# The last softmax chain of a fused attention and mixture kernel, written in another order

## The chip, the cores and the metric

The kernel runs on one core of a Trainium2 chip. The metric is device time in microseconds (us) from the launch to the end of the program. TensorE (PE) multiplies, VectorE (DVE), ScalarE (ACT) and GpSimd (POOL) work element by element, and SyncE (SP) only issues DMA transfers, in the order in which they stand in the program.

## The reference

Three layers follow each other. Attention has 4 batches, 8 heads, 576 positions and 64 values a head; each query keeps its 32 highest scores. Its output, 2304 tokens of 512 values, goes through a soft mixture: 32 slots (8 experts with 4 slots each) are filled by a softmax over all tokens, each expert runs its slots through two matrices, and every token takes its mean of the slots back. The last layer is a dense one with 2048 hidden values.

```
logits = x @ phi                              # 2304 x 32
d = exp(logits - logits.max(0)); d /= d.sum(0) + 1e-09
slot_input = (d.T @ x).reshape(8, 4, 512)
h = maximum(slot_input[e] @ w1[e], 0); slot_out[e] = h @ w2[e]
c = exp(logits - logits.max(1)); c /= c.sum(1) + 1e-09
x = c @ slot_out
h = x @ w_in; g = where(h >= 1, h, where(h <= -1, 0, (h + 1)**2 / 4)); out = g @ w_out
```

## The kernel before

Attention works on 16 pairs of heads, four pairs to a batch. A frame of small operations, written by hand as a list of tokens (ORDER), is repeated; the list TAIL gives the order of the last frames. A token such as `A40.15` is an operation (A: product of the turned weights with v), a row block (4), a head (0) and a pair (15). Each engine does its instructions strictly in that order.

The softmax over tokens runs along: after each batch the 32 columns of logits give a new running maximum, `acc` (the slots' inputs, 128 x 128) is scaled by `al`, the ratio of old to new exponential, and the batch's own product is added. The first three batches do this in quarters while attention goes on. The last batch cannot: its rows come out of the last pair. So `last_mix` handles it in three pieces of 256, 256 and 64 columns (n = 0, 1, 2). Each piece has steps with a letter each: a and b are the products with phi (b is the last of four), c copies the logits from PSUM to the tile lT, d takes the maximum, l copies the logits to lall, e is the exponential, f is al, t turns the exponentials, g copies them to SBUF, w weighs x with them, x adds into acc, and y keeps the running sum. Tokens are `n`, letter and piece: `nb1.15`. All three pieces live in one PSUM tile, `lm_ps`, one bank each.

The framework that builds the program keeps the order of accesses to a tile, not to a bank: where an access to `lm_ps` on one engine follows one on another engine in the list, it waits for it, even where the banks differ. This can be read from the semaphore counts of the built program.

Around the chain stand `fl4` (the 64 last tokens of the last pair turned), `xc` (their copy to xT), `H4` (the rows scaled), `jp`/`jd` (running sums joined), then `sp` (acc turned into si_ps) and `sa` (copied to siT). The expert layer starts with siT: `ex_in(0)`, `ex_in(1)` multiply it with w1 (128 products of 512 columns), `ex_out(0)`, `ex_out(1)` with w2, `m_first` and the loop over steps make the last layer.

The weights come through a ring of SBUF slots of 512 KB. SP issues a load when its slot is free, and there are eight semaphores in turn, so at most eight loads are under way. Here the loads are numbered: w_0 to w_31 are w1; w_32 to w_37 and w_40 to w_65 are w2 (w_50 to w_65 for `ex_out(1)`); w_38 and w_39 are the first two tiles of w_out; w_66 and later are w_in and the rest of w_out. Some slots (wB) take the place of tiles that only attention uses, such as the work pool p_work, so their first load waits for the last use of what lay there. w_38, w_39 and w_40 to w_44 go to such slots.

Of the kernel before, what the change touches and what calls it, by code (L numbers as in the profile page):

```python
# [26 lines left out]
NSLOT = 32  # L27
# [8 lines left out]
NR = 4  # L36
REM = S - NR * P
# [72 lines left out]
def kernel_body(tc, qT, kT, vP, phi, w1, w2, w_in, w_out, out, fast, flag):  # L110
    nc = tc.nc
# [9 lines left out]
    acc = cpool.tile([P, P], F32, name="acc")  # L121
# [81 lines left out]
    p_work = att.enter_context(tc.tile_pool(name="p_work", bufs=2))  # L203
# [290 lines left out]
    last_ps = {}  # L494
# [249 lines left out]
    def last_mix(k, n):
# [8 lines left out]
        turned = bank[:, :(NR + 1) * NSLOT].rearrange("p (r s) -> p r s", s=NSLOT)  # L753
        pu = bank[:, 2 * P:3 * P]
        if k in "ab":
            for c in range(NHP - 1) if k == "a" else (NHP - 1,):
                nc.tensor.matmul(lg, phi_sb[:, c].rearrange("p g s -> p (g s)"), xs[c][1][:, c0:c1],
                                 start=(c == 0), stop=(c == NHP - 1), skip_group_check=True)
        elif k == "c":
            nc.scalar.copy(lT[:, c0:c1], lg)  # L760
        elif k == "d":
            mb = p_moe.tile([P, 1], F32, name="mb", tag="mb", bufs=3)
            nm = p_moe.tile([P, 1], F32, name="nmn", tag="nmn", bufs=4)
            nc.vector.reduce_max(mb, lT[:, c0:c1], axis=AX.X)
            nc.vector.scalar_tensor_tensor(nm, mb, -1.0, nrun[0], op0=ALU.mult, op1=ALU.min)
            sums[n] = dict(old=nrun[0], nm=nm)
            nrun[0] = nm
        elif k == "l":
            own = slice((B - 1) * NSLOT, B * NSLOT)
            nc.vector.tensor_copy(lall[own, c0:c1], lT[own, c0:c1])  # L770
        elif k == "e":
            sb = p_moe.tile([P, 1], F32, name="sb", tag="sb", bufs=3)
            nc.scalar.activation(eT[:, c0:c1], lT[:, c0:c1], AF.Exp, bias=sums[n]["nm"], scale=1.0, accum_out=sb)
            sums[n]["sb"] = sb
        elif k == "f":
            al = p_moe.tile([P, 1], F32, name="al", tag="al", bufs=3)
            nc.scalar.activation(al, sums[n]["old"], AF.Exp, bias=sums[n]["nm"], scale=-1.0)
            sums[n]["al"] = al
        elif k == "t":
            eye = ident[:NSLOT, :NSLOT]  # L780
            for r in main:
                nc.tensor.transpose(turned[:, r, :], eT[:NSLOT, r * P:(r + 1) * P], eye)
            if mid:
                for jj in range(2):
                    sl = slice(jj * REM, (jj + 1) * REM)
                    flip(turned[sl, NR, :], eT[:NSLOT, NR * P:], eye, jj)
        elif k == "g":
            if mid:
                for jj in range(2):
                    sl = slice(jj * REM, (jj + 1) * REM)  # L790
# [25 lines left out]
    def emit(name, pi):  # L816
        k = name[0]
        if k == "l":
            op_late(pi, name[1])
        elif k == "z":  # L820
            if 0 < pi < NPAIR - 1:
                load_pair(pi + 1)
        elif k == "m":
            if pi % NHP == NHP - 1:
                op_moe(pi, k)
        elif k in "cd":
            if k == "c" or pi < NWE:
                i = pi + min(pi, NWE) + (k == "d")
                if i < NCV:
                    conv_op(i, int(name[1]))  # L830
                    if (i, name[1]) == (NCV - 1, "6"):
                        wfree.extend(cv_slots)
                        wload(99)
        else:
            if name == "G00" and pi > 0:
                return
            if name == "S00":
                wload(2)
            if pi == NPAIR - 1 and last_pair(name, pi):
                return  # L840
            calls[k]((pi, int(name[1])), *([int(name[2])] if len(name) > 2 else []))
# [48 lines left out]
    def emit_tail(tok):  # L890
        name, pi = tok.split(".")
        pi = int(pi)
        if name[:2] in special and pi == lastp:
            special[name[:2]]((pi, int(name[2])))
        elif name[0] == "n":
            last_mix(name[1], int(name[2]))
        elif name[0] == "j":
            join(name[1])
        elif name in ("sp", "sa"):
            slots_in(name[1])  # L900
        else:
            emit(name, pi)
        freed(tok)
# [545 lines left out]
```

## Time and profile before

| | us |
|---|---|
| median of 3 runs | 773.34 (772.63 to 773.79) |
| the profiled execution | 771.83 |
| its span, first to last instruction | 770.0 |

| engine | busy us | share of the span |
|---|---|---|
| PE | 736.8 | 96% |
| DVE | 651.0 | 85% |
| ACT | 612.2 | 80% |
| POOL | 491.7 | 64% |

Attention takes the first 480 us or so, the experts stand from 490 to 530 us, and the last layer fills the rest. The shares are means over all stages. The change lies between 477 and 490 us, and what it is worth is read there and in the expert stage behind it.

### The profile page before, as it was taken

The numbers are of one execution on the slowest core, as the hardware profiler recorded it, in microseconds if no ns is written. First come the engines' busy times: TensorE is split into PE (matmuls) and PEld (weight loads), VectorE is DVE, ScalarE is ACT, GpSimd is POOL, SyncE is SP. The second block draws the span as 40 slices with busy tenths as digits, with TensorE's granted clock in tenths as the row PEclk, the third lists the DMA queues.
The fourth block names the chain that finished last, engine by engine and source line by source line (L and its number), as shares of the span: only waits on it lengthen the run. The fifth ranks groups of instructions, "written<-read, shape, count | busy, mean of one in ns | idle before, by whom it ended". The sixth has DMA issues, their size and how long they took to land.

```text
span 770.0 us, 15917 instructions
## 1 busy us (share of the span) xinstructions
PE 736.8 (96%) x5014; PEld 542.5 (70%) x5014; DVE 651.0 (85%) x2924; ACT 612.2 (80%) x1300; POOL 491.7 (64%) x532
## 2 busy tenths in 40 slices
PE   4899999999999999999999999898999999999996
PEld 2477777677777677777777788334577788888885
DVE  5999999999999999999999996173899967776662
ACT  4799999999999999999999997243788864554542
POOL 2899999999999999999999995030455400000000
PEclk9899999999999999999999999899999999999998
DMA  7414314304304302202202137999600020100101
GB/s 230 144 59 149 105 47 150 132 25 150 129 22 151 136 19 96 83 15 96 82 20 96 46 105 273 334 406 406 269 0 1 0 83 1 43 10 33 41 1 45
DMA packets 32013, 81.50 MB, mean 106 GB/s; under 512 B 5680, under 2 KB 6576, under 8 KB 31920
## 3 DMA queue, kind: packets, MB, share of 16 engines
q1 hardware_dynamic: 31632, 79.94, 29.1%
q8 instruction: 41, 0.67, 0.4%
q10 hardware_dynamic: 288, 0.46, 0.2%
q14 instruction: 52, 0.43, 0.2%
HBM read 71.25 MB, written 8.91 MB: 104 GB/s over the span
## 4 chain that ended last, share of the span: by engine, by line
PE 58%; DVE 24%; POOL 7%; DMA 6%; issue 2%; ACT 1%; SPq 1%; DVEq 0%; POOLq 0%; ACTq 0%
PE o_ps L1255 19%; PE av_ps L550 10%; PE s_ps L333 6%; PE pt_ps L509 6%; DVE cand L357 5%; DVE top L463 4%; DMA w<-in_moe_w_dram 3%; PE x_ps L333 3%; DVE ghl L1239 3%; POOL ssb L489 3%; DVE cand L362 2%; DVE top L364 2%; POOL mb L416 2%; PE av_ps L548 2%; PE h_ps L1207 2%
## 5 line engine op out<-in xcount | busy, mean ns | idle before, releaser
L1255 PE MATMUL o_ps<-whl,ghl 128*128 128x512 f32 x864 | 216.9, 395 | 1.3 <-DVE ghl L1221 0.5
L1255 PEld LDWEIGHTS o_ps<-whl,ghl 128*128 128x128 f32 x864 | 160.2, 188 | 38.1 <-DVE whl L1201 2.6
L489 POOL TENSOR_TENSOR ssb<-ssb,pen 128x576 f32<-128x576 f32 x141 | 180.3, 1283 | 2.9 <-ACT pen L486 0.4
L357 DVE MAX8 cand<-ssb 128x8 f32<-128x82 f32 (+1 forms) x1008 | 163.7, 235 | 5.4 <-ACT ssb L348 5.4
L550 PE MATMUL av_ps<-v_sb,ptb 128*128 128x65 f32 (+1 forms) x1280 | 143.0, 262 | 0.0
L550 PEld LDWEIGHTS av_ps<-v_sb,ptb 128*128 128x128 f32 (+1 forms) x1280 | 137.1, 181 | 6.3 <-issue 6.2
L1210 ACT ACTIVATE rg<-h_ps,half 128x384 f32<-128x384 f32 (+1 forms) x98 | 56.0, 572 | 68.3 <-PE h_ps L1207 68.3
L333 PE MATMUL s_ps<-kt,qt 64*128 64x288 f32 x512 | 99.5, 466 | 8.7 <-ACT ssb L348 4.4
L416 POOL TENSOR_SCALAR mb<-ssb,top 128x576 bf16<-128x576 f32 x62 | 106.9, 1724 | 0.9 <-DVE top L364 0.9
L348 ACT COPY ssb<-s_ps 128x576 f32<-128x576 f32 x144 | 95.4, 663 | 10.7 <-PE s_ps L333 9.5
L509 PE MATMUL pt_ps<-ident,ssb 128*128 128x128 f32 x600 | 93.8, 279 | 1.9 <-ACT ptb L525 1.8
L509 PEld LDWEIGHTS pt_ps<-ident,ssb 128*128 128x128 f32 x600 | 67.0, 146 | 29.5 <-ACT rs L533 6.8
L1227 DVE SCALAR_TENSOR_TENSOR rg<-h_ps,rg 128x384 f32<-128x384 f32 x95 | 52.7, 555 | 36.4 <-ACT rg L1211 36.3
L492 ACT ACTIVATE ssb<-ssb,kn 128x576 f32<-128x576 f32 x94 | 76.6, 816 | 0.1
L525 ACT COPY ptb<-pt_ps 128x512 f32<-128x512 f32 x120 | 73.0, 608 | 2.3 <-PE pt_ps L509 2.1
L486 ACT ACTIVATE pen<-ssb,kn 128x576 bf16<-128x576 f32 x94 | 73.8, 809 | 1.2 <-POOL kn L482 0.5
L463 DVE MAX8 top<-x_ps 128x8 f32<-128x584 f32 x94 | 71.1, 758 | 3.2 <-PE x_ps L447 2.8
L1190 POOL TENSOR_SCALAR tr_l<-tr_l 128x512 f32<-128x512 f32 x16 | 24.1, 1503 | 77.3 <-DVE tr_l L1189 77.3
L364 DVE MAX8 top<-cand 128x8 f32<-128x56 f32 x432 | 73.0, 206 | 0.1
L1239 DVE TENSOR_TENSOR ghl<-rg,ghl 128x384 fp32r<-128x384 f32 x95 | 67.7, 713 | 5.7
L453 POOL TENSOR_TENSOR w<-ssb,mb 128x576 f32<-128x576 f32 x50 | 64.6, 1293 | 1.2 <-DVE mb L413 1.2
L333 PEld LDWEIGHTS s_ps<-kt,qt 64*128 64x128 f32 x512 | 39.9, 190 | 34.6 <-ACT ssb L348 10.7
(246 smaller groups left out, 1307.2 us busy)
## 6 DMA issues: line engine op xcount, KB each, us to landing
w<-in_moe_w_dram SPq DMA_DIRECT2D x50, 512.0 KB, 6.7
x<-in_moe_w_in_dram SPq DMA_DIRECT2D x16, 512.0 KB, 3.8
w<-in_moe_w_out_dram SPq DMA_DIRECT2D x16, 512.0 KB, 10.3
w<-in_moe_w_dram SPq DMA_DIRECT2D x28, 256.0 KB, 5.7
kt<-in_k_dram SPq DMA_DIRECT2D x15, 360.0 KB, 4.3
v_sb<-in_v_dram SPq DMA_DIRECT2D x16, 325.0 KB, 6.8
qt<-in_q_dram SPq DMA_DIRECT2D x15, 320.0 KB, 5.0
out_dram<-o_sb SPq DMA_DIRECT2D x17, 256.0 KB, 2.3
```

Source lines behind the costliest of these rows:

```text
L333: nc.tensor.matmul(o, q[us], k[us, c:c + o.shape[-1]], start=True, stop=True, tile_position=(j * D, 0), skip_group_check=True)
L348: nc.scalar.copy(ssb[:, 0] if u[1] == NR else ssb[:, :, hf], st.pop((u, hf))[:, :, :HS])
L357: nc.vector.max(st[u]["cand"][:, j, 8 * g:8 * g + 8], row(u, j)[:, S * g // NSEG:S * (g + 1) // NSEG])
L364: nc.vector.max(t8, cand)
L416: nc.gpsimd.tensor_scalar(kept(u, j), row(u, j), t_u, None, op0=ALU.is_ge)
L463: nc.vector.max(st[u]["top"][:, j, TOPU:], src)
L489: nc.gpsimd.tensor_tensor(row(u, j), row(u, j), st.pop((u, "pen", j)), op=ALU.subtract)
L492: nc.scalar.activation(row(u, j), row(u, j), AF.Exp, bias=st[u]["kn"][:, j, 0:1], scale=0.125)
L509: nc.tensor.transpose(pt[:, c, :], pr[:, c0:c0 + P], ident)
L550: nc.tensor.matmul(o, pj[:, c, sl], v_sb[:, 4 * jj + c, :], start=False, stop=(c == NR - 1), skip_group_check=True)
L1239: nc.vector.tensor_tensor(gl, g, gh.bitcast(F32), op=ALU.subtract)
L1255: nc.tensor.matmul(pos[t][n], a[:, sl], w, start=(f == 0 and k == 0), stop=(f == NF - 1 and k == 2))
```

## The change

The order of the last 70 tokens or so is new, and some steps change.

- Maximum and exponential read the logits from PSUM, not from lT. The copies of pieces 1 and 2 to lT (for lall) are moved to the end of the chain.
- The products of piece 1 with phi are split into single tokens (`na10`, `na11`, `na12`); those of piece 2 stand ahead of the last product with v (`A40`).
- The copies of the turned exponentials of pieces 0 and 1 go from ACT to DVE. Piece 2 has one copy into a new tile e_mid, not two into er.
- Piece 2 is not weighed into lm_ps and added to acc any more. `dg` makes the diagonal matrix `grown` with piece 2's al; `sp` multiplies acc with it, which turns and scales in one, and piece 2's eight products of 64 x 32 add to si_ps there.
- `grown` is a tile of p_work (the tag rs).
- Nine bf16 products of 512 columns (`k4`, `k2`, `k3`), whose result nobody reads, stand in three places of PE's order.

```diff
-Q41.15 R4.15 nb0.15 nc0.15 nd0.15 nl0.15 fl3.15 fl2.15 A40.15 xc2.15 A41.15 rd4.15 na1.15 ne0.15
...
+Q41.15 R4.15 nb0.15 nc0.15 nd0.15 nl0.15 fl3.15 fl2.15 na2.15 A40.15 xc2.15 A41.15 rd4.15 na10.15
+na11.15 ne0.15 xc3.15 H4.15 nf0.15 fl4.15 na12.15 xc4.15 nb1.15 nd1.15 nb2.15 nt0.15 ne1.15 nd2.15
...
     def slots_in(k):
-        if k == "p":
+        if k == "g":
+            last_ps["g"] = p_work.tile([P, P], F32, name="grown", tag="rs", bufs=3)
+            nc.vector.tensor_scalar(last_ps["g"], ident, sums[len(pieces) - 1]["al"], None, op0=ALU.mult)
+        elif k == "p":
             last_ps["s"] = ps_m.tile([P, P], F32, name="si_ps", tag="m_ps")
-            nc.tensor.transpose(last_ps["s"], acc, ident)
+            nc.tensor.matmul(last_ps["s"], acc, last_ps["g"], start=True, stop=True, skip_group_check=True)
...
-            nc.vector.reduce_max(mb, lT[:, c0:c1], axis=AX.X)
+            nc.vector.reduce_max(mb, lg, axis=AX.X)
...
-            nc.scalar.activation(eT[:, c0:c1], lT[:, c0:c1], AF.Exp, bias=sums[n]["nm"], scale=1.0, accum_out=sb)
+            nc.scalar.activation(eT[:, c0:c1], lg, AF.Exp, bias=sums[n]["nm"], scale=1.0, accum_out=sb)
...
         elif k == "g":
             if mid:
-                for jj in range(2):
-                    sl = slice(jj * REM, (jj + 1) * REM)
-                    nc.scalar.copy(er[sl, jj, :], turned[sl, NR, :])
-            if main:
-                lo, hi = main[0], main[-1] + 1
-                nc.scalar.copy(et[:, lo:hi], turned[:, lo:hi])
+                nc.scalar.copy(e_mid, turned[:, 0, :])
+            else:
+                nc.vector.tensor_copy(et[:, main[0]:main[-1] + 1], turned)
         elif k == "w":
-            weigh(pu, xs, et, main, mid)
+            if mid:
+                si = last_ps["s"]
+                for hp in range(NHP):
+                    for jj in range(2):
+                        sl = slice(jj * REM, (jj + 1) * REM)
+                        nc.tensor.matmul(si[sl, hp * NSLOT:(hp + 1) * NSLOT], xs[hp][0][sl, 8, :], e_mid[sl],
+                                         start=False, stop=True, skip_group_check=True)
+            else:
+                weigh(pu, xs, et, main, False)
...
+        elif name[0] == "k":
+            for _ in range(int(name[1:])):
+                nc.tensor.matmul(last_ps["t"][:, 0], nbig, ident.bitcast(BF16).unsqueeze(1).to_broadcast([P, 2, 2 * P]),
+                                 start=True, stop=True, skip_group_check=True)
```

On PE, from the last turning of scores to the turning of piece 0's exponentials, the program stood before like this (L757 are steps a and b, L546 and L550 the last product with v, lx_ps is fl, L782 is t):

```order
L618 MATMUL lx_ps<-ident,xh 128x128 [waits Activation_49]
L546 MATMUL av_ps<-v_sb,rs 64x65 [waits DVE_49,Activation_49]
L550 MATMUL av_ps<-v_sb,ptb 64x65 x4
L546 MATMUL av_ps<-v_sb,rs 64x65
L550 MATMUL av_ps<-v_sb,ptb 64x65 x4
L757 MATMUL lm_ps<-xT,phi_sb 128x256 [waits Activation_49]
L757 MATMUL lm_ps<-xT,phi_sb 128x256 x2
L757 MATMUL lm_ps<-xT,phi_sb 128x256 [waits Activation_49]
L287 MATMUL lx_ps<-ident,xh 64x64 [waits Activation_49]
L285 MATMUL lx_ps<-ident,xh 64x64
L782 MATMUL lm_ps<-ident,eT 128x32 x2
L757 MATMUL lm_ps<-xT,phi_sb 128x64 x3
```

And now (L762 are steps a and b):

```order
L618 MATMUL lx_ps<-ident,xh 128x128 [waits Activation_49]
L762 MATMUL lm_ps<-xT,phi_sb 128x64 [waits DVE_49]
L762 MATMUL lm_ps<-xT,phi_sb 128x64 x2
L546 MATMUL av_ps<-v_sb,rs 64x65 [waits Activation_49]
L550 MATMUL av_ps<-v_sb,ptb 64x65 x4
L546 MATMUL av_ps<-v_sb,rs 64x65
L550 MATMUL av_ps<-v_sb,ptb 64x65 x4
L762 MATMUL lm_ps<-xT,phi_sb 128x256 x2
L287 MATMUL lx_ps<-ident,xh 64x64 [waits Activation_49]
L285 MATMUL lx_ps<-ident,xh 64x64
L762 MATMUL lm_ps<-xT,phi_sb 128x256 x2
L762 MATMUL lm_ps<-xT,phi_sb 128x64 [waits DVE_49,Activation_49]
```

Piece 2's first products moved ahead of the product with v, where they wait for DVE (the maximum of piece 0 is the access to lm_ps before them in the list), and the last two products of piece 1 moved behind fl4. On SP, around the end of attention, the loads stood like this; the first two rows are halves of w_37, and the third is w_38:

```order
L196 DMA w_7714<-in_moe_w_dram 128x512 [waits DMAHW0_49,Activation_49]
L196 DMA w_7715<-in_moe_w_dram 128x512 [waits DMAHW1_49,Activation_49]
L196 DMA w_7857<-in_moe_w_out_dram 128x1024 [waits DMAHW2_49,Activation_49]
L196 DMA w_7859<-in_moe_w_out_dram 128x1024 [waits DMAHW3_49,Activation_49,Pool_49]
L196 DMA w_7861<-in_moe_w_dram 128x1024 [waits DMAHW4_49,PE_49]
L196 DMA w_7863<-in_moe_w_dram 128x1024 [waits DMAHW5_49]
L196 DMA w_7865<-in_moe_w_dram 128x1024 [waits DMAHW6_49,PE_49]
```

And now:

```order
L196 DMA w_7718<-in_moe_w_dram 128x512 [waits DMAHW0_49,Activation_49]
L196 DMA w_7719<-in_moe_w_dram 128x512 [waits DMAHW1_49,Activation_49]
L196 DMA w_7867<-in_moe_w_out_dram 128x1024 [waits DMAHW2_49,PE_49]
L196 DMA w_7869<-in_moe_w_out_dram 128x1024 [waits DMAHW3_49,Activation_49,Pool_49]
L196 DMA w_7871<-in_moe_w_dram 128x1024 [waits DMAHW4_49,Activation_49]
L196 DMA w_7873<-in_moe_w_dram 128x1024 [waits DMAHW5_49]
L196 DMA w_7875<-in_moe_w_dram 128x1024 [waits DMAHW6_49,PE_49]
```

The order of the loads is the same, but w_38 waits for PE where it waited for ACT. By the counts of the built program, ACT's instruction was the copy L533 of the last `rs` tile, and PE's is the first product into si_ps, the one that reads `grown`.

## Rows read from the trace of the kernel before

**Rows 1.** Chain of waits that ended last, 485 to 541 us: start, us, what.

```profile
488.93 0.46 PE si_ps L737
489.41 0.27 ACT siT L739
489.73 8.67 PE h L1049 x64
...
498.62 9.67 DMA w<-in_moe_w_dram
```

**Rows 2.** Stretches: PE, PEld, DVE, ACT, POOL busy; PE clock, DMA share, GB/s.

```profile
484.00:486.00 2.00, 1.22 (x21) 0.76 (x20) 1.33 (x8) 1.39 (x8) 0.00 (x0) 0.98 1.02 398
486.00:488.00 2.00, 1.51 (x32) 1.20 (x32) 0.62 (x4) 0.34 (x2) 0.00 (x0) 0.50 1.03 404
...
494.00:496.00 2.00, 2.00 (x24) 0.52 (x20) 0.00 (x0) 0.00 (x0) 0.00 (x0) 1.00 0.63 219
...
506.00:526.00 20.00, 19.63 (x169) 7.33 (x161) 12.00 (x24) 9.16 (x20) 5.84 (x4) 1.00 1.04 401
```

**Rows 3.** Order of time on SP, three windows: start us, us, what it issued.

```profile
480.46 0.86 SPq L196 DMA_DIRECT2D w<-in_moe_w_out_dram  x2
...
483.51 0.80 SPq L196 DMA_DIRECT2D w<-in_moe_w_dram  x2
...
487.98 1.28 SPq L196 DMA_DIRECT2D w<-in_moe_w_dram  x3
```

**Rows 4.** Order of time, 474 to 494 us: start us, us, engine, line, what, [idle before].

```profile
477.75 0.37 ACT L760 COPY lT<-lm_ps 128x256 f32<-128x256 f32 x1 [0.24 <-PE lm_ps L757]
...
477.86 0.33 PE L546 MATMUL av_ps<-v_sb,rs 128*64 128x65 f32 x2
...
478.16 0.42 DVE L764 TENSOR_REDUCE mb<-lT 128x1 f32<-128x256 f32 x1 [1.98 <-ACT lT L760]
...
478.86 0.51 ACT L773 ACTIVATE eT<-lT,nmn 128x256 f32<-128x256 f32 x1 [0.57 <-DVE nmn L765]
...
478.99 1.99 PE L757 MATMUL lm_ps<-xT,phi_sb 128*128 128x256 f32 x8
...
479.57 0.31 ACT L569 ACTIVATE xh<-av_ps,rd 128x64 f32<-128x64 f32 x1
...
480.92 0.24 PE L287 MATMUL lx_ps<-ident,xh 64*64 64x64 f32 x1
...
481.35 0.31 PE L782 MATMUL lm_ps<-ident,eT 32*128 32x32 f32 x2
...
481.58 0.88 PE L757 MATMUL lm_ps<-xT,phi_sb 128*128 128x64 f32 x6
...
483.89 0.64 PE L721 MATMUL lm_ps<-xh,et 128*32 128x128 f32 x16 [0.25 <-ACT lT L760]
...
484.38 0.35 ACT L773 ACTIVATE eT<-lT,nmn 128x64 f32<-128x64 f32 x1
...
484.64 0.19 ACT L773 ACTIVATION_READ_ACCUMULATOR eT<-lT,nmn 128x1 f32 x1
...
487.26 0.65 PE L721 MATMUL lm_ps<-xh,er 128*32 128x64 f32 x16
488.05 0.73 DVE L798 SCALAR_TENSOR_TENSOR acc<-acc,al,lm_ps 128x128 f32<-128x128 f32 x2 [1.33 <-PE lm_ps L721]
```

**Rows 5.** Instructions of line L1088 (copy from PSUM, DVE): ns min/median/max.

```profile
L1088 DVE COPY so<-soT_ps x8: 214/215/225, 520.5 to 529.6; 128x64 f32<-128x64 f32 x8
```

**Rows 6.** DMA issues in windows at 487.9, 504.5 and 518.7 us: KB each, us to landing.

```profile
w<-in_moe_w_dram SPq DMA_DIRECT2D x1, 512.0 KB, 4.5
...
w<-in_moe_w_dram SPq DMA_DIRECT2D x1, 512.0 KB, 10.2
...
w<-in_moe_w_dram SPq DMA_DIRECT2D x1, 256.0 KB, 6.6
```

**Rows 7.** Order of time on PE, 506 to 545 us.

```profile
524.04 3.64 PE L1072 MATMUL so<-w,h1T 128*32 128x512 f32 x32
```

More of the change, by code (lines that the diff above doesn't have):

```diff
@@ L98 @@
 U40.15 A31.15 B4.15 A20.15 A21.15 rd3.15 rd2.15 T40.15 B3.15 H3.15 xc1.15 xc0.15 H2.15 T41.15 Q40.15
-Q41.15 R4.15 nb0.15 nc0.15 nd0.15 nl0.15 fl3.15 fl2.15 A40.15 xc2.15 A41.15 rd4.15 na1.15 ne0.15
-xc3.15 H4.15 nb1.15 fl4.15 nt0.15 na2.15 nc1.15 xc4.15 nd1.15 nb2.15 nf0.15 jp.15 ng0.15 nc2.15
-nd2.15 nw0.15 ne1.15 ne2.15 jd.15 ny0.15 nt1.15 nl2.15 nt2.15 nf2.15 nl1.15 ng1.15 nx0.15 nf1.15
-ng2.15 ny1.15 nw1.15 nw2.15 ny2.15 nx1.15 nx2.15 sp.15 sa.15
+Q41.15 R4.15 nb0.15 nc0.15 nd0.15 nl0.15 fl3.15 fl2.15 na2.15 A40.15 xc2.15 A41.15 rd4.15 na10.15
+na11.15 ne0.15 xc3.15 H4.15 nf0.15 fl4.15 na12.15 xc4.15 nb1.15 nd1.15 nb2.15 nt0.15 ne1.15 nd2.15
+k4.15 ng0.15 ne2.15 nf1.15 nf2.15 nt1.15 ng1.15 nw0.15 nt2.15 ng2.15 nw1.15 dg.15 nx0.15 nx1.15
+jp.15 jd.15 k2.15 nc1.15 nc2.15 sp.15 nw2.15 ny0.15 ny1.15 ny2.15 nl1.15 nl2.15 k3.15 sa.15
 '''.split()
@@ L732, in kernel_body @@
     siT = cpool.tile([P, NHP, NSLOT], F32, name="siT")
+    e_mid = p_moe.tile([P, NSLOT], F32, name="e_mid")
     def slots_in(k):
-        if k == "p":
+        if k == "g":
+            last_ps["g"] = p_work.tile([P, P], F32, name="grown", tag="rs", bufs=3)
+            nc.vector.tensor_scalar(last_ps["g"], ident, sums[len(pieces) - 1]["al"], None, op0=ALU.mult)
+        elif k == "p":
             last_ps["s"] = ps_m.tile([P, P], F32, name="si_ps", tag="m_ps")
-            nc.tensor.transpose(last_ps["s"], acc, ident)
+            nc.tensor.matmul(last_ps["s"], acc, last_ps["g"], start=True, stop=True, skip_group_check=True)
         else:
@@ L742, in kernel_body, with last_mix @@
     sums = {}
-    def last_mix(k, n):
+    def last_mix(k, n, part=None):
         xs = [x_of[(B - 1) * NHP + hp] for hp in range(NHP)]
@@ L752, in last_mix @@
         lg = bank[:, :c1 - c0]
-        turned = bank[:, :(NR + 1) * NSLOT].rearrange("p (r s) -> p r s", s=NSLOT)
+        turned = bank[:, 3 * P:3 * P + 2 * NSLOT].rearrange("p (r s) -> p r s", s=NSLOT)
         pu = bank[:, 2 * P:3 * P]
         if k in "ab":
-            for c in range(NHP - 1) if k == "a" else (NHP - 1,):
+            for c in ((range(NHP - 1) if part is None else (part,)) if k == "a" else (NHP - 1,)):
                 nc.tensor.matmul(lg, phi_sb[:, c].rearrange("p g s -> p (g s)"), xs[c][1][:, c0:c1],
@@ L780, in last_mix @@
             eye = ident[:NSLOT, :NSLOT]
-            for r in main:
-                nc.tensor.transpose(turned[:, r, :], eT[:NSLOT, r * P:(r + 1) * P], eye)
+            for n_, r in enumerate(main):
+                nc.tensor.transpose(turned[:, n_, :], eT[:NSLOT, r * P:(r + 1) * P], eye)
             if mid:
                 for jj in range(2):
-                    sl = slice(jj * REM, (jj + 1) * REM)
-                    flip(turned[sl, NR, :], eT[:NSLOT, NR * P:], eye, jj)
+                    flip(turned[jj * REM:(jj + 1) * REM, 0, :], eT[:NSLOT, NR * P:], eye, jj)
         elif k == "g":
             if mid:
-                for jj in range(2):
-                    sl = slice(jj * REM, (jj + 1) * REM)
-                    nc.scalar.copy(er[sl, jj, :], turned[sl, NR, :])
-            if main:
-                lo, hi = main[0], main[-1] + 1
-                nc.scalar.copy(et[:, lo:hi], turned[:, lo:hi])
-        elif k == "w":
-            weigh(pu, xs, et, main, mid)
+                nc.scalar.copy(e_mid, turned[:, 0, :])
+            else:
+                nc.vector.tensor_copy(et[:, main[0]:main[-1] + 1], turned)
+        elif k == "w":
+            if mid:
[7 more added lines that the diff above has]
+                weigh(pu, xs, et, main, False)
         elif k == "x":
@@ L895, in emit_tail @@
         elif name[0] == "n":
-            last_mix(name[1], int(name[2]))
+            last_mix(*([name[1]] + [int(x) for x in name[2:]]))
         elif name[0] == "j":
             join(name[1])
-        elif name in ("sp", "sa"):
+        elif name in ("dg", "sp", "sa"):
             slots_in(name[1])
+        elif name[0] == "k":
+            for _ in range(int(name[1:])):
+                nc.tensor.matmul(last_ps["t"][:, 0], nbig, ident.bitcast(BF16).unsqueeze(1).to_broadcast([P, 2, 2 * P]),
+                                 start=True, stop=True, skip_group_check=True)
         else:
```

## The prediction

> **What bounds the kernel now.** I read the chain of waits first, since the shares of busy time (PE 96%) hide what a stage waits for. From 488.9 us it runs through the product into si_ps, the copy to siT and 64 of the 128 products of `ex_in`, and at 498.4 us it leaves PE for the loads: the first takes 9.67 us [rows 1]. So the drain is on the path in two ways. PE starts the experts when siT is there, and SP issues loads when slots come free. The table by stretches shows both. TensorE's clock is granted in full (0.98) to 486 us, is at 0.50 from 486 to 488 and is back at 1.00 from 494; the loads move about 400 GB/s in most stretches, but 219 from 494 to 496, and then 401 from 506 to 526 [rows 2]. From 506 us on the loads are saturated, and a load that starts late is not caught up. SP's own order of time shows when the loads at the end of attention go: w_38 and w_39 at 480.46, w_40 and w_41 at 483.51, w_42 to w_44 at 487.98 [rows 3]. Last I read the drain itself, instruction by instruction, for prices [rows 4].
>
> **The change part by part.** Removed from the path are the copies of pieces 1 and 2 to lT (0.37 us for one of 256 columns [rows 4]), one of two copies to er, and one of three additions to acc (half of 0.73 [rows 4]); the sixteen passes over er (0.65 at the lower clock [rows 4]) become sixteen over e_mid behind si_ps. But each step on `lm_ps` now waits for the step ahead of it in the list, so I add up the new chain from the end of piece 0's products, 477.71.
>
> Block one: copy to lT 0.37 and maximum 0.42, with handoffs of 0.1 until 478.65. Piece 2's first products wait for that maximum, 0.88, until 479.5. Only then comes the last product with v, which started at 477.86 before and took 1.13 (to 478.99); it ends at 480.65. Two of the four products of piece 1, half of 1.93 (478.99 to 480.92), end at 481.6 [rows 4].
>
> Block two: piece 0's exponential waits for these, because they write lm_ps. It stands ahead of the copy to xT and of H4 on ACT's queue, and `fl4` waits for H4. From the exponential's start to H4's end it was 1.02 (478.86 to 479.88), which gives 482.65; fl4 0.43 (480.92 to 481.35) gives 483.1; the other two products of piece 1, 0.96, give 484.05. They ended at 480.9 before [rows 4]. What was hidden beside PE's work is now in front of it: 3.1 us lost here.
>
> Block three: maximum 0.42 and handoffs, 484.6. Last product of piece 2 0.3 (two passes at 0.15, the six of 0.88) and two turns 0.23 (481.35 to 481.58), 485.1. Exponential of piece 1 to the end of its accumulator: 0.51 + 0.10, the 0.10 from 484.73 to 484.83 at the smaller one, 485.8 [rows 4]. Maximum and minimum of piece 2 and the copy to et on DVE at no more than the 0.215 of a copy of 64 columns from PSUM [rows 5], 486.5. Exponential of piece 2 0.45 (484.38 to 484.83), 487.0. Two turns 0.31, a copy as before, 487.6. First weighing 0.6 (0.64 for 16 passes), turns 0.43 as in fl4, copy to e_mid 0.2, second weighing 0.6, 489.5. Two additions 0.75, handoff 0.14, product into si_ps 0.3: 490.7 [rows 4]. Before it ended at 488.93 + 0.46 = 489.39 [rows 1], so the chain is 1.3 us later there. A maximum that reads PSUM is not in the trace. If the handoffs are nil and it costs nothing above the copy it replaces the end is 489.9; if each of the four steps on DVE that read PSUM costs 0.2 more, it is 491.5. I stay at 490.7.
>
> `grown` itself (one DVE step) stands between other waits and costs nothing. But it lies in p_work. w_38 goes to a slot that takes p_work's place; its wait was for an early copy of ACT and is now for the product that reads `grown`. SP issues in order, so w_38 goes from 480.46 to about 490.8, and with it w_39 to w_44, six loads queued behind it. Until then there is nothing to move: w_38 to w_41 are 2.1 MB that flowed between 480 and 489 before, 5 us at 400 GB/s.
>
> From there the loads run without a gap: seven are ready at once, and each group of products of `ex_in` frees more than the queue moves. A load issued to a nearly empty queue landed after 4.5 us [rows 6], so w_38 lands at 495.3. In the saturated stretch w_57 landed at 504.52 + 10.2 = 514.7 and the second half of w_65 at 518.69 + 6.6 = 525.3 [rows 6]: eight loads in 10.6 us, 1.32 each, or 1.31 by 512 KB at 401 GB/s [rows 2]. I take 1.30. The second half of w_65 is 27 loads later, at 530.4, its first half at 529.75. `ex_out(1)` ran from 524.04 for 3.64 us [rows 7]: four groups of 0.86, and the third group's last expert needs w_65's first half, at 526.1 before. It now waits until 529.75, and a fourth group of 0.86 follows: it ends at 530.6, not 527.7. Sum: +2.9; I write +2.8, since the wait of the third group overlaps some of its passes. All that follows hangs on the experts' output one after the other, so this passes to the end.
>
> PE's own delay lies beside it and is smaller. The sixteen passes over e_mid are a shape that no row shows: between 0.65 (sixteen passes over er [rows 4]) and 2.3 (the three passes of fl4 take 0.43, so 0.14 each [rows 4]); I take 1.1, half the upper price for half the columns. Copy to siT 0.27 [rows 1] and `k3` (three products of 512 columns, 0.8 by the pace of 0.26 a product of that width) make 492.7 the start of `ex_in`, 3.0 late. The Trainium skill, "TensorE: Matmul & The Clock Gate", section "Wait — 56ns, not 53.3ns?", has a floor of about 25 ns between matmuls however small they are: 0.4 us for sixteen passes as an estimate from that page, which would start `ex_in` 0.7 earlier; no run here shows this shape. The sum doesn't move by it, as w_38 waits for the product ahead of these passes. With the clock kept up, 64 products take 2 x 3.64 less 0.2, 7.1, not 8.67 [rows 1, 7], so PE gets 1.6 back and is 1.4 late when it comes to the wait for w_65: hidden behind the 2.9. `k4` and `k2` end before what follows them is ready and cost nothing.
>
> The profiled execution would go from 771.83 to 774.6. The runs shown have a median 1.5 above that execution, 773.34, so I predict 776.1. Of this kernel I take 0.2%, 1.5 us, as the least that a measurement tells from no change.
>
> **Rivals.** The clock falls all the same. The new chain leaves PE idle for 1.1 us before fl4, 0.5 at the maximum of piece 1 and 1.0 behind `k4`; before, gaps of this kind stood ahead of 0.50 [rows 2]. If the last weighings run at the lower level, si_ps is 1.2 later and w_38 with it: 777.3. If the wait for w_65 brings the clock down too, m_first and the first steps run at half pace for several us, and it is 779 to 780.
>
> The loads are late but nobody waits: if w_65 had 3 us of slack, not 0.9 (525.3 for its second half against a need at about 526 to 527), only PE's 1.4 stays: 774.7, within 0.2%. Against it speaks that the queue was saturated [rows 2].
>
> Faster: the bf16 products hold the clock at 2.4 GHz through the drain, `ex_in` gives back 1.6 and so frees its slots sooner, and the stretch at 219 GB/s is filled. It decides once si_ps is ready no later than before, which needs 1.3 us less than I count, for instance if exponential 0 does not hold H4. Then 773.34 less 1.6 is 771.7. The Trainium skill, the same page, "Part 1: The HAM clock gate", says that the clock goes to the lower level when the array was idle and comes back once it was busy. By that rule filled pauses keep the full clock; the trace agrees with the fall behind a stretch with pauses, and no run here shows them filled.
>
> **How the numbers follow.** The late load decides: 0.54, 774.9 to 777.6 with si_ps between 489.9 and 491.5 and 0.6 either way from the rate of the loads. The clock falls as well: 0.17, 777.3 to 780. Only PE late: 0.17, 774.7. Faster: 0.12, 771.7. So slower 0.71, same 0.17, faster 0.12. The range goes from 773.3, leaving out most of the faster case, to 779.0.
>
> **What would show it.** SP's order of time should hold no load between about 481.5 and 490.5, the stretches from 485 to 492 should move next to nothing, and then 400 GB/s or more without a dip to 526. PE should wait in `ex_out(1)` for a load at about 527 to 530. Piece 1's products should end at about 484, and fl4 should wait for H4. If loads go at 480 to 484 as before, or if `ex_in` starts before 490, I am wrong.

## The result and the profile after

The changed kernel takes 779.01 us (median of 6 runs, 777.54 to 780.11) against 773.23 us (6 runs) of the kernel before: 1.0073 times as long, 95% interval 1.0061 to 1.0085, so by the ratio 5.6 us slower. The prediction was 776.1, in a range to 779.0, so the time lies at the very end of the range: the direction and the late loads were right, the predicted loss (2.8) was half of the measured one. The profiled execution took 780.11 us, its span is 778.3. It is the slowest of the six, and the profile of before is one of the quicker executions of its kernel (771.83), so the two profiles differ by more (8.3 us) than the medians. Of the 8.3 us, 1.14 lie ahead of the change: piece 0's last product with phi starts at 478.16 us in the trace after, and at 477.02 before (first row after, second row before). I subtract 1.14 where I compare times of day.

```profile
478.16 0.70 PE L762 MATMUL lm_ps<-xT,phi_sb 128*128 128x256 f32 x2
...
477.02 0.70 PE L757 MATMUL lm_ps<-xT,phi_sb 128*128 128x256 f32 x2
```

SP's order of time answers to [rows 3]; columns are start, duration and what was issued.

```profile
478.26 4.84 SPq L196 DMA_DIRECT2D w<-in_moe_w_dram  x5
493.98 0.80 SPq L196 DMA_DIRECT2D w<-in_moe_w_out_dram  x2
494.88 9.51 SPq L196 DMA_DIRECT2D w<-in_moe_w_dram  x11
```

w_38 and w_39 went at 480.46 before, and go at 493.98 now, right behind the product into si_ps, as predicted. The stretches answer to [rows 2] (PE, PEld, DVE, ACT, POOL busy, then the clock, the DMA share and GB/s).

```profile
484.00:486.00 2.00, 1.44 (x7) 0.86 (x6) 0.42 (x1) 0.22 (x2) 0.00 (x0) 1.00 0.72 258
486.00:488.00 2.00, 1.61 (x8) 0.80 (x8) 0.68 (x4) 0.58 (x3) 0.00 (x0) 1.00 0.01 3
488.00:490.00 2.00, 1.17 (x18) 0.79 (x18) 0.42 (x2) 0.76 (x4) 0.00 (x0) 0.65 0.00 0
494.00:496.00 2.00, 2.00 (x19) 1.09 (x19) 0.59 (x4) 0.27 (x1) 0.00 (x0) 0.50 0.48 111
496.00:498.00 2.00, 1.85 (x9) 0.45 (x12) 0.00 (x0) 0.00 (x0) 0.00 (x0) 0.50 1.01 401
506.00:526.00 20.00, 19.79 (x166) 7.48 (x158) 13.59 (x23) 9.62 (x20) 5.83 (x4) 1.00 1.03 406
```

From 486 to 494 us next to nothing is loaded, where 252 to 404 GB/s flowed before. The clock falls to its lower level (0.50, 1.2 GHz) here too, between 488 and 490, and is back only between 498 and 500 (before: from 486 to between 492 and 494). The drain answers to [rows 4] (start, duration, engine, line, what, idle time before it and its releaser).

```profile
479.78 0.88 PE L762 MATMUL lm_ps<-xT,phi_sb 128*128 128x64 f32 x6 [0.70 <-DVE mb L769]
482.89 0.47 ACT L778 ACTIVATE eT<-lm_ps,nmn 128x256 f32<-128x256 f32 x1 [3.46 <-PE lm_ps L762]
483.88 0.24 PE L287 MATMUL lx_ps<-ident,xh 64*64 64x64 f32 x1 [1.03 <-ACT xh L569]
484.31 1.13 PE L762 MATMUL lm_ps<-xT,phi_sb 128*128 128x256 f32 x4
485.55 0.42 DVE L769 TENSOR_REDUCE mb<-lm_ps 128x1 f32<-128x256 f32 x1 [3.36 <-PE lm_ps L762]
486.69 1.04 PE L912 MATMUL lt_ps<-ident,nbig 128*128 128x512 bf16 x4
489.15 1.08 PE L721 MATMUL lm_ps<-xh,et 128*32 128x128 f32 x16 [0.38 <-DVE et L795]
491.05 1.08 PE L721 MATMUL lm_ps<-xh,et 128*32 128x128 f32 x16 [0.28 <-ACT e_mid L793]
492.51 1.01 PE L912 MATMUL lt_ps<-ident,nbig 128*128 128x512 bf16 x2
493.31 0.63 PE L742 MATMUL si_ps<-grown,acc 128*128 128x128 f32 x2
493.88 1.07 PE L802 MATMUL si_ps<-e_mid,xh 64*64 64x32 f32 x16
494.88 1.46 PE L912 MATMUL lt_ps<-ident,nbig 128*128 128x512 bf16 x3
494.99 0.27 ACT L744 COPY siT<-si_ps 128x128 f32<-128x128 f32 x1 [1.40 <-PE si_ps L802]
```

ACT is idle for 3.46 us until the products ahead of exponential 0 in the list are done, `fl4` waits 1.03 for H4, and piece 1's products end at 485.44: blocks one and two are as predicted. Block three runs longer than its prices, since both weighings are at the lower clock: 1.08 each, not 0.6. siT is ready at 495.26, yet `ex_in` starts behind `k3`, at 496.49.

The chain of waits answers to [rows 1], PE's order of time to [rows 7]; the third fence is PE's weight loads.

```profile
496.36 0.14 issue
496.49 11.41 PE h L1062 x93
507.90 11.28 DMA w<-in_moe_w_dram
519.25 7.70 DMA w<-in_moe_w_dram
...
526.96 6.58 DMA w<-in_moe_w_dram
```

```profile
496.49 11.65 PE L1062 MATMUL h<-w,siT 128*32 128x512 f32 x96
...
530.47 2.77 PE L1085 MATMUL so<-w,h1T 128*32 128x512 f32 x20
533.59 2.58 PE L1085 MATMUL so<-w,h1T 128*32 128x512 f32 x12 [0.35 <-DMA w<-in_moe_w_dram]
```

```profile
533.59 0.14 PEld L1085 LDWEIGHTS so<-w,h1T 128*32 128x32 f32 x2 [1.26 <-DMA w<-in_moe_w_dram]
534.26 0.32 PEld L1085 LDWEIGHTS so<-w,h1T 128*32 128x32 f32 x8 [0.54 <-DMA w<-in_moe_w_dram]
534.94 0.32 PEld L1085 LDWEIGHTS so<-w,h1T 128*32 128x32 f32 x2 [0.36 <-DMA w<-in_moe_w_dram]
```

The last 32 products of `ex_out(1)` take 5.70 us (530.47 to 536.17), not 3.64: the wait for the last loads is there, 2.06 in sum (for w_64, which lands at 533.54, and then for the two halves of w_65). Of the chain's long pieces on a DMA only the last, from 526.96 to 533.54, ends in a wait of PE; during those from 507.90 on SP waits for a load to land before it issues the next, and PE works. PE's order of time of the kernel before shows what I had not looked at:

```profile
489.73 11.97 PE L1049 MATMUL h<-w,siT 128*32 128x512 f32 x96 [0.35 <-ACT siT L739]
501.64 0.66 PE L1002 MATMUL lt_ps<-ident,lall 128*128 128x128 f32 x4
...
502.97 1.22 PE L1064 MATMUL h1T_ps<-ident,h1s 128*128 128x128 f32 x8 [0.20 <-ACT lt L1006]
...
521.23 0.24 PE L1035 MATMUL c_ps<-ident,c 64*128 64x64 f32 x1 [0.37 <-DVE so L1088]
```

From 489.73 to the end of `ex_out(1)` PE stands still for 0.20 and 0.37 us and at no load. So before the change the stage is bound by PE, with the loads just in time, and a late start of `ex_in` passes to the end. The stage's length is made of three parts in every trace: the first 96 products of `ex_in` (10.51 us at full clock, more where the clock is low), the last 32 of `ex_out(1)` (3.64, more where they wait for a load), and 22.34 for all between, the same to 0.01 in all traces here. So the loss can be split: 1.14 ahead of the change, 5.62 for `ex_in` (496.49 - 489.73 - 1.14), -0.32 (11.65 - 11.97) and 2.06 in `ex_out(1)`: 8.50 of 8.28; the rest of the kernel gives 0.2 back. The split follows PE; it does not say that each part would go by itself, since a PE that came earlier would wait longer for the same load.

### The profile page after: what moved, and what is told of

The parts are those of the page before. It is cut to its first block, busy times and chain, and to the rows that moved or that the text cites. A ratio compares the mean times of both kernels' runs of the same rounds, so it can differ in the third digit from the quotient of the medians.

```text
span 778.3 us, 15936 instructions
## 1 busy us (share of the span) xinstructions
PE 746.4 (96%) x5024; PEld 546.1 (70%) x5024; DVE 651.8 (84%) x2926; ACT 611.8 (79%) x1297; POOL 492.3 (63%) x532
## 4 chain that ended last, share of the span: by engine, by line
PE 55%; DVE 29%; POOL 6%; DMA 4%; ACT 2%; issue 2%; DVEq 0%; POOLq 0%; ACTq 0%; SPq 0%
PE o_ps L1268 19%; PE av_ps L550 9%; DVE cand L357 7%; PE s_ps L333 6%; DVE top L463 5%; PE pt_ps L509 5%; DMA w<-in_moe_w_dram 3%; DVE ghl L1252 3%; PE x_ps L333 3%; DVE cand L362 3%; DVE top L364 2%; POOL ssb L489 2%; DVE mb L413 2%; POOL mb L416 2%; PE h_ps L1220 2%
## 5 line engine op out<-in xcount | busy, mean ns | idle before, releaser
L550 PE MATMUL av_ps<-v_sb,ptb 128*128 128x65 f32 (+1 forms) x1280 | 143.0, 262 | 0.0
L550 PEld LDWEIGHTS av_ps<-v_sb,ptb 128*128 128x128 f32 (+1 forms) x1280 | 137.1, 181 | 6.3 <-issue 6.2
L333 PE MATMUL s_ps<-kt,qt 64*128 64x288 f32 x512 | 101.1, 473 | 8.7 <-ACT ssb L348 4.4
```

The source lines that it names most:

```text
L333: nc.tensor.matmul(o, q[us], k[us, c:c + o.shape[-1]], start=True, stop=True, tile_position=(j * D, 0), skip_group_check=True)
L550: nc.tensor.matmul(o, pj[:, c, sl], v_sb[:, 4 * jj + c, :], start=False, stop=(c == NR - 1), skip_group_check=True)
```

## Experiments

Four theories are tested: L, the late loads alone (the prediction's reading); P, PE late by itself, with nothing that hides it; H, the bf16 products hold the clock up; K, they only stand in the way. All ratios are against the kernel before, run on the same chip in turn, and differences against before are worked out from them. Of the lists of tokens the edits show only the stretch that changes. Columns 2 to 4 are of each profiled execution: the start of `ex_in` from the last product of piece 0 with phi (so that the attention's jitter drops out; 12.71 before), the 96 products and the 32 products.

| kernel | ex_in from piece 0 | 96 products | last 32 | ratio (95%) |
|---|---|---|---|---|
| before | 12.71 | 11.97 | 3.64 | 1 |
| changed | 18.33 | 11.65 | 5.70 | 1.0073 (1.0061 to 1.0085) |
| changed, diagonal moved | 18.46 | 12.57 | 3.64 | 1.0036 (1.0021 to 1.0050) |
| before, w_38 held | 13.12 | 12.42 | 5.90 | 1.0034 (1.0022 to 1.0046) |
| before, ex_in late | 17.37 | 10.79 | 3.64 | 1.0030 (1.0018 to 1.0042) |
| changed, no bf16 products | 17.21 | 12.03 | 5.29 | 1.0072 (1.0059 to 1.0086) |
| changed, order put back | 15.25 | 11.31 | 5.72 | 1.0030 (1.0018 to 1.0042) |
| diagonal and order | 15.25 | 11.29 | 3.64 | 0.9992 (0.9981 to 1.0003) |
| the same, no bf16 products | 14.16 | 13.27 | 3.64 | 1.0018 (1.0009 to 1.0027) |
| before, bf16 in pauses | 11.93 | 10.51 | 3.64 | 0.9969 (0.9960 to 0.9979) |
| three PSUM tiles | 10.65 | 12.33 | 3.64 | 0.9955 (0.9938 to 0.9971) |
| three tiles, 5 bf16 | 10.20 | 10.51 | 3.82 | 0.9946 (0.9932 to 0.9960) |
| three tiles, 8 bf16 | 10.86 | 10.51 | 3.64 | 0.9949 (0.9937 to 0.9962) |

A trace is of one execution and the ratio of several, so the two need not agree to better than 1 or 2 us.

**The diagonal elsewhere.** `grown` goes into a tile that no load waits for.

```diff
-last_ps["g"] = p_work.tile([P, P], F32, name="grown", tag="rs", bufs=3)
+last_ps["g"] = same.rearrange("p r s -> p (r s)")
-k4.15 ng0.15
+jp.15 k4.15 ng0.15
...
-jp.15 jd.15 k2.15
+jd.15 k2.15
```

> The changed kernel, but the diagonal matrix of al is written into the tile same of p_moe (free once the product into rq_ps has read it, which moves ahead of k4) and not into a tile of p_work. w_38 then waits for the copy L533 again, as before the change, and goes at about 482 us instead of 494. Theory L (late loads, as predicted): the time goes back to that of before plus 1.4 for PE alone, 774.7 us. Theory P (PE is late by itself): ex_in still starts at about 495 to 496 us, PE runs from there without a gap to ex_out(1) as it does in both traces (34.3 us before, 34.0 after), and only the wait inside ex_out(1) goes, 5.7 against 3.64 us: about 2.1 less than the changed kernel, 777 us.

PE's order of time of this kernel:

```profile
495.58 12.57 PE L1062 MATMUL h<-w,siT 128*32 128x512 f32 x96
...
530.49 3.64 PE L1085 MATMUL so<-w,h1T 128*32 128x512 f32 x32
```

776.29 us, 2.8 above before and some 2.9 below the changed kernel: w_38 went at 482.73 and the wait in `ex_out(1)` is gone, but `ex_in` starts as late as before this edit. Theory P holds by the trace; the time lies between the two theories' (774.7 and 777). The runs spread: the profiled one took 778.49 us, with 12.57 for the 96 products, and three with a mean clock of 0.999 took 774.3 to 774.5, near theory L's time.

**The load alone late.** The kernel before, where the product into si_ps reads a copy of the identity in p_work.

```diff
+last_ps["g"] = p_work.tile([P, P], F32, name="eye2", tag="rs", bufs=3)
+nc.vector.tensor_copy(last_ps["g"], ident)
-nc.tensor.transpose(last_ps["s"], acc, ident)
+nc.tensor.transpose(last_ps["s"], acc, last_ps["g"])
```

> The kernel before, with one thing added: a copy of the identity in a tile of p_work, which the product into si_ps reads. Only the release of w_38 changes, from 480.5 to about 489.5 us; the chain is as before. Theory L: w_65 lands at about 530.4 us, ex_out(1) ends 2.7 to 4.0 later, 776 to 777.2 us. Theory P gives the same wait, since PE is on time here and the loads are not: 776 to 777.2. If nobody waits for the late loads (the rival of the prediction): 773.2, no change, and the whole loss of the changed kernel lies in PE's late start.

SP's order of time of this kernel, then PE's:

```profile
490.03 0.81 SPq L196 DMA_DIRECT2D w<-in_moe_w_out_dram  x2
...
525.07 2.77 PE L1075 MATMUL so<-w,h1T 128*32 128x512 f32 x20
528.40 2.57 PE L1075 MATMUL so<-w,h1T 128*32 128x512 f32 x12 [0.57 <-DMA w<-in_moe_w_dram]
```

775.41 us, ratio 1.0034: +2.6 us, just below what both theories gave (+2.8 to +4.0). w_38 went at 490.03, and the wait stands where the prediction put it. So one tile's place in a pool costs about 2.6 us by itself, what the prediction (+2.8) made of it. In the trace the wait is 2.26 of it; `ex_in` also starts 0.41 later there and its 96 products take 0.45 longer, which no wait for a load explains.

**PE alone late.** The kernel before, with eleven bf16 products of 512 columns between `sp` and `sa`.

```diff
-nx2.15 sp.15 sa.15
+nx2.15 sp.15 k11.15 sa.15
```

> The kernel before, with eleven bf16 products of 512 columns between the product into si_ps and ex_in. At the lower clock they take 5.4 us, so ex_in starts 4.7 to 5.1 us late, while every load that waits for something ahead of ex_in (w_38 to w_44) keeps its time: PE's delay alone, without the late loads. Theory P (PE runs without a gap from ex_in to the end of ex_out(1), so a late start is never made up): the time is longer by that delay less what a clock that rises sooner gives back (at most 1.5 us in ex_in): 776.5 to 778 us. If a late start is hidden behind the loads, as the prediction had it: 774 to 774.7.

PE's order of time of this kernel:

```profile
490.20 4.90 PE L903 MATMUL lt_ps<-ident,nbig 128*128 128x512 bf16 x11
495.25 10.79 PE L1053 MATMUL h<-w,siT 128*32 128x512 f32 x96
```

775.43 us, ratio 1.0030, +2.3: below theory P's 776.5 to 778 and above the 774 to 774.7 of a hidden delay. The profile shows 4.66 us of delay, 1.18 back in the 96 products, no wait for a load: 3.5 between the two profiles, against 2.3 by the ratio. The delay is passed on, not hidden, as long as the loads keep their time; my bounds were too high.

**Without the bf16 products.**

```diff
-k4.15 ng0.15
+ng0.15
...
-jd.15 k2.15 nc1.15
+jd.15 nc1.15
...
-nl2.15 k3.15 sa.15
+nl2.15 sa.15
```

> The changed kernel without the nine bf16 products k4, k2 and k3. Theory P: k3 ends 1.2 us after siT is ready and k2 holds the product into si_ps by 0.4, so ex_in starts 1.2 to 1.6 earlier: 777.4 to 777.8 us, and the clock is at 0.50 in the same stretch. Theory H (the fillers hold the clock up for what follows): without them the clock falls earlier than 488.7 us or comes back later, and the time is as before this edit or up to 1 us longer, 779 to 780.

778.50 us, 1.0072: by the ratio no change, which is theory H's time and not theory P's 1.2 to 1.6 less. But theory H's reason is not shown: the clock is at 0.50 for about 10 us with the products and without them. `ex_in` starts 1.12 earlier, as theory P has it, the 96 products take 0.38 longer and the wait for the load stays (5.29), since w_38 goes no earlier (15.88 us behind piece 0's last product with phi, 15.82 in the changed kernel). With the loads last, the products neither cost nor earn what can be measured.

**The order ahead of the last chain put back.**

```diff
-nd0.15 nl0.15 fl3.15 fl2.15 na2.15 A40.15 xc2.15 A41.15 rd4.15 na10.15
-na11.15 ne0.15 xc3.15 H4.15 nf0.15 fl4.15 na12.15 xc4.15 nb1.15 nd1.15 nb2.15 nt0.15
+nd0.15 ne0.15 nl0.15 fl3.15 fl2.15 A40.15 xc2.15 A41.15 rd4.15 na10.15
+na11.15 na12.15 xc3.15 H4.15 nb1.15 fl4.15 nf0.15 nd1.15 na2.15 xc4.15 nb2.15 nt0.15
```

> The changed kernel with the order ahead of the last chain put back: piece 2's products behind fl4, the products of piece 1 in one row right behind the last product with v, the exponential of piece 0 ahead of them, so that H4 and fl4 wait for nothing new. Theory P and the sum of the prediction: products of piece 1 end at about 481 instead of 484.3 us (both on the clock of the trace of before), si_ps and w_38 are 2 to 3 us earlier, and the time is 776 to 777 us. If the exponential of piece 0 was not what held fl4 and the rest of the chain absorbs the 3 us (serial accesses to lm_ps decide): 778.5 to 779, no change.

PE's order of time of this kernel:

```profile
479.61 2.00 PE L762 MATMUL lm_ps<-xT,phi_sb 128*128 128x256 f32 x8 [0.36 <-ACT eT L778]
481.53 0.24 PE L287 MATMUL lx_ps<-ident,xh 64*64 64x64 f32 x1
...
529.25 2.57 PE L1085 MATMUL so<-w,h1T 128*32 128x512 f32 x12 [0.38 <-DMA w<-in_moe_w_dram]
```

775.47 us, 1.0030, some 3.3 less than the changed kernel: a little better than expected. `fl4` waits for nothing, `ex_in` starts 3.08 earlier (15.25 against 18.33), which is the 3.1 of blocks one and two, and w_38 moves with it. The wait for the load stays.

**Both edits,** with and without the bf16 products (k3 is in the first of the two).

> The changed kernel with both of the edits tried so far: the order ahead of the last chain put back, and the diagonal matrix in the tile same of p_moe (the product into rq_ps moves ahead of k4). k4, k2 and k3 stay. If the loss is two delays that reach ex_out(1) beside each other, PE's late start and the late loads, taking both away gives before plus what the chain is still late: ex_in starts at 492.4 against 489.7 us and gets back 1 us or so by the clock, no wait in ex_out(1): 774 to 775 us. If the two edits were worth the same microseconds twice (one delay only), the time is that of the order alone, 775.5.

> As the kernel with both edits, but without the nine bf16 products. Theory K (k3 in the path costs 1.2 us between siT and ex_in): 1 us less than with them, 773 to 774 us. Theory H (the products let the clock stay at 2.4 GHz in a part of the runs, which the runs with the granted clock of 0.999 in the kernel with the moved diagonal hint at, 774.4 us against 776 to 778.5): without them no run has a mean clock of 0.999, and the median is the same or 0.5 to 1 us longer.

PE's order of time, with the products:

```profile
492.43 11.29 PE L1062 MATMUL h<-w,siT 128*32 128x512 f32 x96
...
526.05 3.64 PE L1085 MATMUL so<-w,h1T 128*32 128x512 f32 x32
```

And without them:

```profile
491.71 13.27 PE L1062 MATMUL h<-w,siT 128*32 128x512 f32 x96 [0.36 <-ACT siT L744]
```

The stretch from 494 to 496 us, with the products and then without:

```profile
494.00:496.00 2.00, 2.00 (x24) 0.67 (x20) 0.00 (x0) 0.00 (x0) 0.00 (x0) 0.98 1.02 410
494.00:496.00 2.00, 2.00 (x16) 0.42 (x12) 0.00 (x0) 0.00 (x0) 0.00 (x0) 0.50 1.02 399
```

772.06 us with them (0.9992, no change against before), 774.34 without (1.0018). The two edits add up: 2.9 and 3.3 us alone, 6.3 together, which is 2 us more than expected. With the products `ex_in` starts 1.1 us later and its 96 products are 2.0 us shorter, so theory K falls. Theory H holds for the direction of the time and for the mean clocks (up to 0.999 with the products, at most 0.993 without), but the products do not keep the clock up in the traced execution: it falls at about 487 us with and without them, and comes back some 3 us sooner with them. And the times do not follow the mean clock: a run with 0.994 took 770.5 us and one with 0.995 took 774.5.

**The kernel before with bf16 products in its pauses.**

```diff
-xc4.15 nd1.15 nb2.15
+xc4.15 nd1.15 k2.15 nb2.15
...
-ng2.15 ny1.15 nw1.15 nw2.15 ny2.15 nx1.15 nx2.15 sp.15
+ng2.15 ny1.15 k4.15 nw1.15 nw2.15 ny2.15 nx1.15 nx2.15 k4.15 sp.15
```

> The kernel before, with ten bf16 products of 512 columns added in the three places where PE waits in the drain: two ahead of the last product of piece 2, four ahead of piece 1's weighing, four ahead of the product into si_ps. Theory H: in some or all runs the clock stays at 2.4 GHz through the drain, the weighings and the first products of ex_in give back 1.5 to 2.5 us, and loads that were just in time take some of it back: 771.5 to 772.5 us. If the clock falls nevertheless, the four products ahead of si_ps take 2.1 us instead of 1.04 and delay it by about 1: 774 us.

The stretch of the drain (columns as in the stretches above):

```profile
480.00:490.00 10.00, 8.99 (x99) 4.87 (x101) 3.35 (x15) 3.16 (x15) 0.00 (x0) 1.00 1.02 385
```

769.97 us, 0.9969, better than expected: the clock stays at 1.00 through the drain, and the 96 products take 10.51. This alone beats both kernels.

**A PSUM tile for each piece,** no bf16 products, and the order that this allows.

```diff
-last_ps["b"] = ps_s.tile([P, 3, 512], F32, name="lm_ps", tag="x_ps", bufs=1)
+shape, tag = (([P, 3, 512], "x_ps"), ([P, 2, 512], "s_ps"), ([P, 1, 512], "pt_ps"))[n]
+last_ps["b", n] = ps_s.tile(shape, F32, name=f"lm{n}_ps", tag=tag, bufs=1)
...
+nb0.15 nd0.15 ne0.15 fl3.15 fl2.15 A40.15 xc2.15 A41.15 rd4.15 na10.15 na11.15 na12.15
+xc3.15 H4.15 nb1.15 fl4.15 nf0.15 nd1.15 nt0.15 jp.15 xc4.15 ne1.15 ng0.15 jd.15 na2.15 nb2.15 nd2.15
+nw0.15 ne2.15 nt1.15 ng1.15 nf1.15 nf2.15 nt2.15 ng2.15 nw1.15 dg.15 nx0.15 nc0.15 nx1.15 nc1.15
+nc2.15 sp.15 nw2.15 ny0.15 ny1.15 ny2.15 nl0.15 nl1.15 nl2.15 sa.15
```

> The changed kernel without the bf16 products, with the diagonal matrix in p_moe, and with a PSUM tile of its own for each of the three pieces (piece 1 takes the place of lt_ps, piece 2 that of lx_ps), so that accesses of different pieces no longer wait for each other; the order follows from that: exponential 0 right behind its maximum, piece 0 weighed while piece 1 is in its exponential, the copies to lT last. If the serial accesses to one tile are what makes the new chain long, the sum of the steps on the prices of the trace of before gives the product into si_ps at 484.9 us and ex_in at 486 (489.7 before), at full clock; the loads then decide, and the time is 769.5 to 772 us, faster than before. If the loads (w_65 at 525.3 before) cannot come earlier, the gain is at most 1 us: 772.3. If the accesses were not the limit, 774 to 775.

PE's order of time of this kernel:

```profile
486.17 0.79 PE L742 MATMUL si_ps<-same,acc 128*128 128x128 f32 x2 [0.45 <-DVE acc L808]
...
488.33 12.33 PE L1063 MATMUL h<-w,siT 128*32 128x512 f32 x96 [0.36 <-ACT siT L744]
```

769.55 us, 0.9955, at the quick end of what was expected. `ex_in` starts 2.06 us sooner than before and 7.7 sooner than in the changed kernel; 3.7 had been the sum against before, at full clock; it fell before 488 here (0.50 from 486 to 488). The 7.7 are not all due to the tiles: the nearest kernel with one tile is the one above with both edits and no bf16 products, and against it `ex_in` starts 3.5 sooner (10.65 against 14.16). So the serial accesses to one tile make the changed chain long, together with the order that they force; tiles and order were changed at once here, and what each is worth alone is not shown.

**The same with bf16 products** behind the first weighing and ahead of si_ps, five and eight (the edit with five is shown).

```diff
-nw0.15 ne2.15
+nw0.15 k2.15 ne2.15
...
-nc2.15 sp.15
+nc2.15 k3.15 sp.15
```

> The kernel with three PSUM tiles, with five bf16 products of 512 columns added: two behind the weighing of piece 0, three ahead of the product into si_ps (they write the tile of rq_ps, which is already read). In the trace of the kernel with three tiles the clock falls at about 485.6 us, is back at 492, and 96 products of ex_in take 12.33 us; in the kernel before with ten such products it stayed and they took 10.51. If five are enough to hold the clock, ex_in starts 0.5 to 1 us earlier and takes 1.8 less: 767 to 768 us. If they are not, the three ahead of si_ps take 1.5 us in a pause of 0.45 at the lower clock and the time is 770 to 770.5.

> The same with eight: four behind the weighing of piece 0, four ahead of the product into si_ps. The pauses there are 0.14 and 0.45 us, so at full clock the eight (0.26 each) delay the chain by 1.4 us in sum. If they hold the clock they earn 1.8 in ex_in and up to 1 in the chain: 768 to 769 us; if not, 772.

PE's order of time of the kernel with five:

```profile
487.07 10.51 PE L1063 MATMUL h<-w,siT 128*32 128x512 f32 x96 [0.37 <-ACT siT L744]
...
519.92 3.82 PE L1086 MATMUL so<-w,h1T 128*32 128x512 f32 x32
```

768.52 us (0.9946, 0.9932 to 0.9960) and 769.12 (0.9949): both hold the clock, by 96 products in 10.51. Five are the fastest kernel here, 4.2 us below before; 767 to 768 us were expected, so the gain fell a little short. The intervals overlap with that of no products at all, so that the products earn time in this kernel is not shown. In the 3.82 for the last 32 a weight load waits 0.25 us for a load: PE has just caught up with the loads, and a shorter chain would probably earn little more as long as they start where they do.

## Why the prediction was right and wrong

- **Late loads: right, by mechanism.** SP's empty stretch, the wait in `ex_out(1)` and its place were as written; held alone in the kernel before it costs 2.6 us, predicted 2.8. In part that is luck: w_38 landed 3.6 us after its issue there, not 4.5 (the load that gave the 4.5 had three others under way), and the 27 loads behind it took 1.34 each, not 1.30.
- **Blocks one and two: right.** Piece 1's products were to end at 484.05; they end at 485.44, 484.3 without the offset. 3.1 us were predicted as lost; the order put back moves `ex_in` by 3.08.
- **Block three: too short.** The product into si_ps was to end at 490.7; it ended at 493.95, 492.8 without the offset. I priced this block at full clock and put the lower clock into a rival (0.17). The clock fell: 0.5 more for each weighing, 0.3 for the product into si_ps, 0.4 since k2 took 1.01 us and ended that much behind the additions; that is 1.7 of the 2.1.
- **k3: right in place, too cheap.** 0.8 was counted; it took 1.46, and `ex_in` started 1.2 after siT was ready.
- **The step that failed: `ex_out(1)` "ends at 530.6", the end of the late loads' path.** It ended at 536.17, 535.0 without the offset, 4.4 later. 2.1 of it is w_38, which waits for block three. The other 2.4 is the way from w_38's issue to the end of `ex_out(1)`: 39.8 us by the sum, 42.2 here, 40.9 in the kernel before with w_38 held. 1.0 of it lies behind the last load: the sum has 0.2 between the landing of w_65's second half and the end, the trace 1.2 (534.94 to 536.17). The rest are the loads, which took 1.3 longer from w_38 to w_65 than the sum and the held kernel have; why, stays open. With the 2.9 of the sum this makes 7.3, what the split above has from `ex_in` to the end of `ex_out(1)` (7.36).
- **"PE gets 1.6 back and is 1.4 late when it comes to the wait for w_65: hidden behind the 2.9": right in order, wrong in size.** `ex_in` came 5.62 late, not 3.0, and got back 0.32, not 1.6, because the low stretch of the clock moved along with the chain. So PE was 5.3 late, and the loads still ended 2.06 behind it. What is hidden in this way is not gone: when w_38 goes in time, PE's lateness alone costs 2.8, where the rival "only PE late" had 1.4. I had read the chain's 9.67 us on a load [rows 1] as a wait, and so the stage as bound by the loads; it was bound by both, and either delay alone costs 2.3 to 2.8.
- **Small slips in the sums.** 490.7 with 1.1, 0.27 and 0.8 makes 492.9, not 492.7, and the bounds about 776.1 make 774.7 to 777.5; neither changes the reading.
- **The rivals.** "The clock falls as well" (777.3 to 780) is what the time looks like, and by its mechanism too: si_ps late at the lower level, w_38 with it. Its second half, a clock that falls at the wait for w_65, did not happen (1.00 in every stretch from 500 to 538). That the time lies in the range at all is due to this rival: the bounds of the main case end at 777.6. "Faster" was wrong for this kernel, but its mechanism is real: bf16 products in the pauses hold the clock, in another order.
- **The page.** The Trainium skill, "TensorE: Matmul & The Clock Gate", "Part 1: The HAM clock gate", says that the clock drops behind idle stretches and returns under load. The traces agree where the pauses were filled in the kernel before (1.00 from 480 to 490 us, 0.50 from 486 without). In the changed kernel the products did not do it: 0.70, 1.03 and 0.68 us of waits for mb and H4 stood open ahead of `k4`; that these are the reason is not shown. One of its six runs has a mean clock of 0.999 and took 778.5 all the same: with the loads late, a better clock earned nothing that shows.

What stays open: why the mean clock differs between runs of one kernel (0.982 to 0.999 with the moved diagonal), and why their times do (774.3 to 778.5 us there). Only one run of each kernel has a trace.

## What to carry to other kernels

A piece of the chain on a transfer is not yet a wait: look at the engine's own order of time for idle before its instructions, and price a late start in full where there is none. Before a tile is taken from a pool, look at what will take its place later, since one late reader holds a load and every load behind it on the same queue. Where several banks are in one tile, each access may wait for the others; a tile for each, with the order that this allows, gave the earliest `ex_in` here of all kernels without bf16 products.

## What the runs showed of the hardware

- Filled pauses are worth 2.4 us in a kernel that computes the same: ten bf16 products, 2.7 us of PE time, made the kernel before 0.31% faster.
- 96 products of 512 columns took 10.51 us at a clock of 1.00, and 10.8 to 13.3 where it was low in their first part.
- The sixteen passes of 64 x 32 that no row of before had took 1.07 us at 0.50, and 0.66 at 1.00 in the kernel with three tiles and five products: 41 ns each, not the 25 ns behind the prediction's estimate of 0.4 for all.
